# Scores of block-causal attention as three rounded products, from batch 2 on

## The chip, the cores and the metric

The kernel runs on one core of a Trainium2 chip. The metric is the device time of one execution in microseconds. A core has a matrix engine (TensorE, PE in the profile, its weight loads PEld), three engines that work elementwise (VectorE or DVE, ScalarE or ACT, GpSimd or POOL), and SyncE (SP), which here only issues DMAs. Each engine works through its own instructions in order and waits on semaphores for the others. TensorE reads SBUF and writes PSUM, which has 8 banks of 128 rows x 512 f32 values.

## The reference

Attention over 8 batches, 8 heads, 576 positions and a head size of 64, with a mask by blocks of 64; then a feed-forward layer that is gated by a product over positions:

```python
scores = scale * np.matmul(q, k.transpose(0, 1, 3, 2))
mask = block_i >= block_j            # block = pos // 64
scores = np.where(mask, scores, -1000000000.0)
scores = scores - np.max(scores, axis=-1, keepdims=True)
attn = np.exp(scores)
attn = attn / (np.sum(attn, axis=-1, keepdims=True) + 1e-09)
x = np.matmul(attn, v)               # heads side by side: 576 x 512

h = np.maximum(x @ w_in, 0.0)        # 512 -> 1024
u, v = (h[..., :512], h[..., 512:])
v_n = (v - mean(v)) / np.sqrt(var(v) + 1e-06)
v_s = np.einsum('ts,bsd->btd', w_spatial, v_n) + b_spatial[None, :, None]
return (u * v_s) @ w_out             # 512 -> 512
```

## The kernel before

Heads are worked in pairs: head 0 of a pair lies in rows 0 to 63, head 1 in rows 64 to 127, so there are 4 pairs a batch and 32 in all. `raw` holds keys (columns 0 to 575) and queries (576 to 1151) of a pair, head size in the rows. Its pool has two buffers.

Query positions are cut in four tiles `t` = 0 to 3 of 128 and a rest of 64. Tile `t` needs the first 128 (t + 1) keys. `scores_run` (L577) makes the four tiles of a pair with `raw` as f32: for each tile and head one matmul, with 128 queries as the stationary operand and the keys streaming, so 128 to 512 columns with 64 rows. Tiles 3 and 2 take a PSUM bank for each head, tiles 1 and 0 share one. Banks are taken in turn from a ring of six (`bank`, L398), which also serves the rest's scores (`scores_8`, L518, matmuls at L444) and the product with `v` (`av_pair`, L665). Then `top` (L409) takes the maximum with the mask on VectorE (L416) and the exponential on ScalarE (L423), `norm` (L500) divides on GpSimd (L514), and `turn_blocks` (L618) transposes blocks of 32 on VectorE; DMAs on SyncE regroup the result (L652, L660) for `av_pair`.

The feed-forward layer (`moe`, L698) splits each operand into a rounded part and a remainder, both fp32r, and adds three products: rounded with rounded, rounded with remainder, remainder with rounded. Its groups are `v_group` (`mv`, 12 matmuls of 512 columns, 8 for the last), `u_group` (`mu`, 12 of 288), `sp_group` (`ms`, 14 of 288) and `out_group` (`mo`, 12 of 288). Each takes one of two banks (`ps_m`). In `sp_group` VectorE multiplies (L830), ScalarE rounds to `gh` (L833), and a subtraction gives `gl` (L834): on GpSimd for the first three of four groups, on VectorE for the last. `out_group` uses that last part in its last matmul.

From pair 5 on the main loop (L1042) works one pair at a time: `scores_run` of pair g, `av_pair` of pair g - 1, then some 7 or 8 groups of the layer of a batch before, with transposes and regrouping between them. `issue` (L1029) puts out one group, then `follow` (L1023) advances the later stages of the groups before. The rest's scores of pair g + 1 come among the last groups, and after them SyncE loads `v` of pair g + 1 and `raw` of pair g + 2 (L1076 to L1079). `in_order` (L224) fixes each engine's order to that of the program text. By their place in the batch, a pair's groups are: pair 0 the second half's output groups of the batch before that, `v` 0 and 4, `u` 0; pair 1 `v` 1 to 3 and `u` 1 to 4; pair 2 `u` 5 to 7 and the first half's spatial groups; pair 3 the first half's output groups and the second half's spatial groups. Batch 0 differs: its first two output groups stand right behind its first spatial groups, in the stretch of the third pair.

Of the kernel before, what the change touches and what calls it, by code (L numbers as in the profile page):

```python
# [10 lines left out]
F32 = mybir.dt.float32  # L11
F32R = mybir.dt.float32r
I32 = mybir.dt.int32
AF = mybir.ActivationFunctionType
ALU = mybir.AluOpType
PSUM = bass.MemoryType.PSUM

P = 128
S = 576
# [36 lines left out]
def kernel(  # L56
# [10 lines left out]
    nc = tc.nc  # L67
    B, NPAIR = qk.shape[0], qk.shape[1]
# [4 lines left out]
    ND = DH // P  # L73
# [5 lines left out]
    raw_p = ctx.enter_context(tc.tile_pool(name="raw_p", bufs=2))  # L79
# [5 lines left out]
    ff_p = ctx.enter_context(tc.tile_pool(name="ff_p", bufs=1))  # L85
# [122 lines left out]
    raws = {}  # L208

    def load_pair(b, pr):  # L210
        raw = raw_p.tile([P, KQ], F32, tag="raw", name=f"raw_{b}_{pr}")
        if b == 0 and pr == 0:
            for cs in (slice(0, 256), slice(S, S + 256), slice(256, S), slice(S + 256, KQ)):
                nc.sync.dma_start(raw[:, cs], qk[b, pr, :, cs])
        else:
            nc.sync.dma_start(raw, qk[b, pr])
        raws[(b, pr)] = raw


    traced = nc.cur_bb.bb  # L220
# [18 lines left out]
    mm = nc.tensor.matmul  # L239
# [158 lines left out]
    def bank(nm):  # L398
        pool, tag = RING[turn[0] % len(RING)]
        turn[0] += 1  # L400
        return pool.tile([P, 512], F32, tag=tag, name=nm)
# [7 lines left out]
    def top(st, t, hd, p, parts):  # L409

        k = PLACE[(t, hd)]
        at = 0
        for m, ps in enumerate(parts):
            n = ps.shape[1]
            mk = mask[:, 512 - n:] if t < 8 else mask[:, :n]
            nc.vector.tensor_tensor_reduce(  # L416
                out=p[:, at:at + n], in0=ps, in1=mk, scale=-0.125,
                scalar=BIG if m == 0 else st[:, k:k + 1], op0=ALU.add, op1=ALU.min,
                accum_out=st[:, k + m:k + m + 1],
            )  # L420
            at += n
        mx = st[:, k + len(parts) - 1:k + len(parts)]
        nc.scalar.activation(  # L423
            p, p, AF.Exp, bias=mx, scale=-1.0, accum_out=st[:, 10 + k:11 + k]
        )
# [74 lines left out]
    def norm(st, tiles):  # L500
        if tiles[0][0] == 8 and len(tiles) == 2:
            return norm_8(st)
        k0 = PLACE[tiles[0][:2]]
        ks = slice(10 + k0, 10 + k0 + len(tiles))
        rs = slice(20 + k0, 20 + k0 + len(tiles))
        n = len(tiles)
        sums, to = st[:, ks], st[:, 32:32 + n]
        if n > 1:
            sums, to = thrice(sums), three(st[:, 32:32 + 3 * n])
        nc.vector.tensor_scalar(out=to, in0=sums, scalar1=EPS_SM, scalar2=None, op0=ALU.add)  # L510
        nc.vector.reciprocal(st[:, rs], st[:, 32:32 + n])  # L511
        for t, hd, p in tiles:
            k = 20 + PLACE[(t, hd)]
            nc.gpsimd.tensor_scalar(  # L514
                out=p, in0=p, scalar1=st[:, k:k + 1], scalar2=1.0, op0=ALU.mult, op1=ALU.mult
            )
# [60 lines left out]
    def scores_run(b, pr):  # L577


        raw = raws.pop((b, pr))  # L580
        st = stats.pop((b, pr))
        ps = {}
        for t in (3, 2, 1, 0):
            for hd in range(2):
                js = slice(64 * hd, 64 * hd + 64)
                n = P * (t + 1)
                if t:
                    bk = bank(f"s{t}_{b}_{pr}_{hd}")
                    ps[(t, hd)] = bk[:, :n]
                    if t == 1:  # L590
                        ps[(0, hd)] = bk[:, n:n + P]
                mm(  # L592
                    ps[(t, hd)], raw[js, S + t * P:S + (t + 1) * P], raw[js, :n],
                    start=True, stop=True,
                )
        due = None
        for ts in ((3,), (2,), (1, 0)):
            tiles = []
            for hd in range(2):
                p = (p_big if ts[0] == 3 else p_small)(f"p{ts[0]}_{b}_{pr}_{hd}")  # L600
                at = 0
                for t in ts:
                    n = P * (t + 1)
                    p_of[(b, pr, t, hd)] = p[:, at:at + n]
                    top(st, t, hd, p[:, at:at + n], [ps[(t, hd)]])
                    tiles.append((t, hd, p[:, at:at + n]))
                    at += n
            if due:
                norm(st, due)
            due = tiles  # L610
        turn_blocks(b, pr, 8, 0)
        turn_blocks(b, pr, 3, 0)
        norm(st, due)
# [84 lines left out]
    def moe(b):  # L698
# [102 lines left out]
        g = {}  # L801

        def sp_group(z, dc):
            if dc == 0:
                if b == B - 1 and z:

                    t = pt_tile("pb", "g_last", F32R)[:, :2 * ND * HT]
                    t = t.rearrange("p (x d t) -> p x d t", x=2, d=ND)
                    g[z] = (t[:, 0], t[:, 1])
                else:  # L810
                    g[z] = (
                        ff_p.tile([P, ND, HT], F32R, tag="gh", name=f"gh_{b}_{z}"),
                        ff_p.tile([P, ND, HT], F32R, tag="gl", name=f"gl_{b}_{z}"),
                    )
            gh, gl = g[z]
            ps = ps_m.tile([P, 512], F32, tag="m", name=f"ms_{b}_{z}_{dc}")
            zs = slice(z * HT, (z + 1) * HT)
            ds = slice(dc * P, (dc + 1) * P)
            n = 0
            for k in range(FULL):  # L820
                vh, vl = vn[k]
                for (a, w) in ((vh, ws_hi), (vh, ws_lo), (vl, ws_hi)):
                    mm(  # L823
                        ps[:, :HT], a[:, ds], w[:, k, zs], start=(n == 0), stop=False
                    )
                    n += 1
            mm(ps[:, :HT], vs_a[:, ds], ws_a[:, zs], start=False, stop=False)  # L827
            mm(ps[:, :HT], vs_b[:97, ds], ws_b[:97, zs], start=False, stop=True)  # L828
            uz = u_tile()[:, dc, zs]
            nc.vector.tensor_tensor(out=uz, in0=ps[:, :HT], in1=uz, op=ALU.mult)  # L830
            if dc < ND - 1:
                yield
            nc.scalar.copy(gh[:, dc, :], uz)  # L833
            (nc.vector if dc == ND - 1 else nc.gpsimd).tensor_tensor(  # L834
                out=gl[:, dc, :], in0=uz, in1=gh[:, dc, :].bitcast(F32), op=ALU.subtract
            )
            if dc == ND - 1:
                yield
# [23 lines left out]
        out = [[lambda z=z, e=e: out_group(z, e) for e in range(NO)] for z in range(2)]  # L862
# [17 lines left out]
    pairs = [(b, pr) for b in range(B) for pr in range(NPAIR)]  # L880
# [40 lines left out]

    early = steps.pop(-1)
    load_pair(0, 0)
    load_pair(0, 1)
    load_v(0, 0)
# [103 lines left out]
    def issue(f, last=False):  # L1029

        gen = f()
        if not last and step < 28:
            follow()
        next(gen)
        if not last and step >= 28:
            follow()
        behind.append(gen)
        next_step()

    mlp = moe(0)  # L1040
    rest = []
    for g in range(NPAIR, len(pairs)):  # L1042
        b, pr = pairs[g]
        if g > NPAIR:
            scores_run(b, pr)
            av = av_pair(*pairs[g - 1])
            next(av, None)
            turn_blocks(b, pr, 3, 1)
            next(av, None)
            next(av, None)  # L1050
            if pr != 2:
                follow()
            turn_blocks(b, pr, 2, 0)
        regroup_8(b, pr)
        in_order()
        if pr == 0:
            if g > NPAIR:
                mlp = moe(b - 1)
            groups, rest = rest + mlp[0], mlp[-1]
        else:  # L1060
            groups = mlp[pr]
        ahead = scores_8(*pairs[g + 1]) if g + 1 < len(pairs) else iter([])
        for i, f in enumerate(groups):
            issue(f, pr < 2 and i == len(groups) - 1 and not (pr and g > NPAIR + 1))
            if i == 0:
                turn_blocks(b, pr, 1, 0)
                turn_blocks(b, pr, 0, 0)
                turn_blocks(b, pr, 2, 1)
                turn_blocks(b, pr, 1, 1)
                turn_blocks(b, pr, 0, 1)  # L1070
            if i == 1:
                regroup(b, pr)
            if i >= len(groups) - (4 if pr == 0 and g > NPAIR else 3):
                next(ahead, None)
        in_order()
        if g + 1 < len(pairs):  # L1076
            load_v(*pairs[g + 1])
        if g + 2 < len(pairs):
            load_pair(*pairs[g + 2])  # L1079
        in_order()  # L1080
# [61 lines left out]
```

## Time and profile before

| what | us |
|---|---|
| median of 3 runs | 678.1 (677.87 to 678.51) |
| the profiled execution | 677.25 |
| its span in the trace | 675.2 |
| matmuls of the four tiles' scores (L592), 432 records, busy | 65.5 |

The page gives one execution on the chip. Its parts are the busy time of each engine, the span in 40 slices, the DMA queues, the chain of work that ended last (followed back from the last instruction to what released it), the groups of instructions with mean durations, and the DMA issues. In rows of a timeline come the start, the length, the engine with its line, the operation with output and inputs, the shapes, how many were merged, and in brackets the idle time ahead of it with what ended it. The granted clock of TensorE was 0.997 of full speed in this execution.

### The profile page before, as it was taken

Reading aid. Unit: us, or ns where it says so; the run is one execution under the profiler, and the core shown is the slowest. Engines: PE = TensorE matmul, PEld = TensorE weight load, DVE = VectorE, ACT = ScalarE, POOL = GpSimd, SP = SyncE. Lnnn points to the kernel's source line nnn. Section 1 sums busy time; section 2 is a strip of 40 time slices with the busy share of each in tenths; the row PEclk is TensorE's granted clock in tenths of the full one; section 3 lists DMA queues with packets and bytes.
Section 4 is the critical chain, followed back from the end, with each engine's and each line's share of the span. In section 5 each row is a group of like instructions: output and inputs, shape, how many; then the busy total and the mean of one; then the engine's idle time right before and its main releaser. Section 6 shows DMA issues by size and latency. Waiting matters only on the chain.

```text
span 675.2 us, 15538 instructions
## 1 busy us (share of the span) xinstructions
PE 655.9 (97%) x5328; PEld 554.2 (82%) x5328; DVE 482.9 (72%) x1875; ACT 390.8 (58%) x1144; POOL 291.1 (43%) x496
## 2 busy tenths in 40 slices
PE   9887879999999999999999999999999999999998
PEld 5445678888888888988789888888798887999998
DVE  6989899778876687776866788766877768661520
ACT  5977785555943477545754558434775457542632
POOL 4768566343543336442353435433364423640130
PEclk9999989999999999999999999999999999999999
DMA  7534655664557644566656545576445676451002
GB/s 237 164 143 155 190 130 124 177 178 130 143 144 188 155 112 118 160 158 168 152 119 153 147 132 140 146 188 151 111 117 165 153 176 149 113 124 54 0 1 71
DMA packets 51106, 93.45 MB, mean 138 GB/s; under 512 B 5970, under 2 KB 27986, under 8 KB 51028
## 3 DMA queue, kind: packets, MB, share of 16 engines
q1 hardware_dynamic: 41812, 83.03, 48.3%
q10 hardware_dynamic: 9216, 9.44, 4.2%
q8 instruction: 42, 0.69, 0.4%
q14 instruction: 36, 0.29, 0.1%
HBM read 37.13 MB, written 9.44 MB: 69 GB/s over the span
## 4 chain that ended last, share of the span: by engine, by line
PE 74%; DVE 14%; ACT 5%; POOL 3%; issue 2%; SPq 1%; DMA 1%; DVEq 0%; ACTq 0%; POOLq 0%
PE mo L849 16%; PE ms L823 15%; PE mu L793 11%; PE mv L719 8%; PE s L592 8%; PE av L676 7%; DVE p L416 2%; PE s L444 2%; PE mv L730 2%; PE av L688 2%; DVE pb L638 1%; ACT p L423 1%; PE ms L828 1%; PE ms L827 1%; DVE x L329 1%
## 5 line engine op out<-in xcount | busy, mean ns | idle before, releaser
L514 POOL TENSOR_SCALAR p<-p,sst 128x256 f32<-128x256 f32 (+4 forms) x244 | 130.8, 555 | 93.1 <-DVE sst L511 71.3
L423 ACT ACTIVATE p<-p,sst 128x256 f32<-128x256 f32 (+4 forms) x244 | 134.7, 553 | 32.3 <-DVE sst L416 32.2
L793 PE MATMUL mu<-x,wi_hi 128*128 128x288 f32 x512 | 110.9, 300 | 3.4 <-ACT u L798 3.4
L416 DVE CUSTOM_DVE_ANT_0 p<-s,mask 128x512 f32<-128x512 f32 (+1 forms) x216 | 92.5, 484 | 1.3 <-PE s L592 0.7
L793 PEld LDWEIGHTS mu<-x,wi_hi 128*128 128x128 f32 x512 | 85.2, 190 | 8.4 <-ACT u L798 3.9
L638 DVE STREAM_TRANSPOSE pb<-p 128x384 f32<-128x384 f32 (+1 forms) x224 | 89.3, 443 | 0.3 <-POOL p L514 0.3
L719 PE MATMUL mv<-wi_hi,x 128*128 128x512 f32 x256 | 86.9, 401 | 2.4 <-DVE x L329 1.0
L834 POOL TENSOR_TENSOR gl<-u,gh 128x288 fp32r<-128x288 f32 x45 | 36.2, 804 | 112.8 <-ACT gh L833 112.8
L773 POOL TENSOR_TENSOR vl<-vr,vh 128x512 fp32r<-128x512 f32 x32 | 41.3, 1291 | 90.8 <-ACT vh L772 90.8
L830 DVE TENSOR_TENSOR u<-ms,u 128x288 f32<-128x288 f32 x64 | 29.2, 456 | 68.5 <-PE ms L828 68.5
L823 PE MATMUL ms<-ws_hi,vh 128*128 128x288 f32 x256 | 77.1, 301 | 0.2 <-DVE u L830 0.2
L823 PE MATMUL ms<-ws_hi,vl 128*128 128x288 f32 x256 | 75.6, 295 | 0.0
L823 PE MATMUL ms<-ws_lo,vh 128*128 128x288 f32 x256 | 75.4, 294 | 0.0
L793 PE MATMUL mu<-x,wi_lo 128*128 128x288 f32 x256 | 70.4, 297 | 0.0
L676 PE MATMUL av<-ptt,v 128*64 128x64 f32 (+3 forms) x896 | 67.5, 303 | 1.8 <-DVE sst L416 1.8
L676 PEld LDWEIGHTS av<-ptt,v 128*64 128x64 f32 x896 | 53.4, 137 | 15.5 <-DVE sst L416 2.0
L592 PE MATMUL s<-raw 64*128 64x384 f32 (+3 forms) x432 | 65.5, 442 | 0.0
L719 PEld LDWEIGHTS mv<-wi_hi,x 128*128 128x128 f32 x256 | 47.9, 188 | 17.5 <-ACT o L855 2.6
L592 PEld LDWEIGHTS s<-raw 64*128 64x128 f32 x432 | 39.5, 186 | 25.5 <-issue 14.5
L484 ACT ACTIVATE p<-p,sst 128x288 f32<-128x288 f32 x56 | 29.6, 529 | 52.4 <-DVE sst L469 52.3
L855 ACT COPY o<-mo 128x288 f32<-128x288 f32 x64 | 25.6, 399 | 59.3 <-PE mo L849 53.5
L833 ACT CAST gh<-u 128x288 fp32r<-128x288 f32 x60 | 24.3, 428 | 57.3 <-DVE u L830 57.3
(161 smaller groups left out, 1474.3 us busy)
## 6 DMA issues: line engine op xcount, KB each, us to landing
ptt<-pb SPq DMA_DIRECT2D x112, 320.0 KB, 6.1
raw<-qk SPq DMA_DIRECT2D x31, 576.0 KB, 6.3
v<-v SPq DMA_DIRECT2D x32, 320.0 KB, 5.1
outT<-o ACTq DMA_DIRECT2D x64, 144.0 KB, 2.6
ptt<-pb SPq DMA_DIRECT2D x112, 80.0 KB, 2.3
r_gh<-w_in SPq DMA_DIRECT2D x3, 512.0 KB, 4.0
r_gl<-w_in SPq DMA_DIRECT2D x3, 512.0 KB, 3.6
rs<-w_spT SPq DMA_DIRECT2D x4, 288.0 KB, 4.6
```

What stands on the lines that cost most here:

```text
L416: nc.vector.tensor_tensor_reduce(out=p[:, at:at + n], in0=ps, in1=mk, scale=-0.125, scalar=BIG if m == 0 else st[:, k:k + 1], op0=ALU.add, ...
L423: nc.scalar.activation(p, p, AF.Exp, bias=mx, scale=-1.0, accum_out=st[:, 10 + k:11 + k])
L514: nc.gpsimd.tensor_scalar(out=p, in0=p, scalar1=st[:, k:k + 1], scalar2=1.0, op0=ALU.mult, op1=ALU.mult)
L592: mm(ps[(t, hd)], raw[js, S + t * P:S + (t + 1) * P], raw[js, :n], start=True, stop=True,)
L638: nc.vector.transpose(to(hd * XH + 32 * t, [[96, m], *dims] if m > 1 else dims), p[:, :m * P])
L676: mm(to[js, :, 32 * c:], vt[:, c, js], ptt[:, 2 * z:2 * z + 2, at:at + P - 32 * c], start=(c == 0), stop=(c == 3),)
L719: mm(ps, xs[k][:, j, cs], w[:, k, DH:], start=(n == 0), stop=(n == 3 * NC - 1),)
L773: nc.gpsimd.tensor_tensor(out=vl, in0=vr, in1=vh.bitcast(F32), op=ALU.subtract)
L793: mm(ps[:, :HT], w[:, k, ds], xs[k][:, j, zs], start=(n == 0), stop=(n == 3 * NC - 1),)
L823: mm(ps[:, :HT], a[:, ds], w[:, k, zs], start=(n == 0), stop=False)
L834: (nc.vector if dc == ND - 1 else nc.gpsimd).tensor_tensor(out=gl[:, dc, :], in0=uz, in1=gh[:, dc, :].bitcast(F32), op=ALU.subtract)
L849: mm(ps[:, :HT], w[:, k, es], a[:, k, :], start=(n == 0), stop=(n == 3 * ND - 1),)
```

## The change

Pairs 8 to 31 (batch 2 on) get their keys and queries split ahead of their scores. `split_pair` rounds the first 512 keys and queries to fp32r on ScalarE (`hi`), and GpSimd (queries) and VectorE (keys) subtract to get the remainders (`lo`). `hi` lies in the buffer `rw`, which the weights' decoding uses early in the run; `lo` takes a turn in the pool of `raw`. The split of pair g + 1 is put out while pair g's groups run: ahead of the second group in pair 0 of a batch, ahead of the third in the others. `scores_run` then makes three products for each tile and head, which add up in the bank; the two heads alternate within each product. The scores of the rest (`matmuls_8`) still read `raw`. Besides, the last `gl` of `sp_group` moves from VectorE to GpSimd in every batch but the last.

```diff
+    parts = {}
+
+    def split_pair(b, pr):
+
+        hi = ff_p.tile([P, 2, 512], F32R, tag="rw", name=f"hi_{b}_{pr}")
+        lo = raw_p.tile([P, 2, 512], F32R, tag="raw", name=f"lo_{b}_{pr}")
+        raw = raws[(b, pr)].rearrange("p (x s) -> p x s", x=2)[:, :, :512]
+        nc.scalar.copy(hi, raw)
+        for x, engine in ((1, nc.gpsimd), (0, nc.vector)):
+            engine.tensor_tensor(
+                out=lo[:, x], in0=raw[:, x], in1=hi[:, x].bitcast(F32), op=ALU.subtract
+            )
+        parts[(b, pr)] = hi, lo
...
         raw = raws.pop((b, pr))
         st = stats.pop((b, pr))
+        qk = [(raw[:, S:], raw)]
+        if (b, pr) in parts:
+            hi, lo = parts.pop((b, pr))
+            qk = [(x[:, 1], y[:, 0]) for x, y in ((hi, hi), (hi, lo), (lo, hi))]
         ps = {}
         for t in (3, 2, 1, 0):
-            for hd in range(2):
-                js = slice(64 * hd, 64 * hd + 64)
-                n = P * (t + 1)
-                if t:
-                    bk = bank(f"s{t}_{b}_{pr}_{hd}")
-                    ps[(t, hd)] = bk[:, :n]
-                    if t == 1:
-                        ps[(0, hd)] = bk[:, n:n + P]
-                mm(
-                    ps[(t, hd)], raw[js, S + t * P:S + (t + 1) * P], raw[js, :n],
-                    start=True, stop=True,
-                )
+            n = P * (t + 1)
+            for m, (q, k) in enumerate(qk):
+                for hd in range(2):
+                    js = slice(64 * hd, 64 * hd + 64)
+                    if t and m == 0:
+                        bk = bank(f"s{t}_{b}_{pr}_{hd}")
+                        ps[(t, hd)] = bk[:, :n]
+                        if t == 1:
+                            ps[(0, hd)] = bk[:, n:n + P]
+                    mm(
+                        ps[(t, hd)], q[js, t * P:(t + 1) * P], k[js, :n],
+                        start=(m == 0), stop=(m == len(qk) - 1),
+                    )
...
-            (nc.vector if dc == ND - 1 else nc.gpsimd).tensor_tensor(
+            (nc.vector if dc == ND - 1 and b == B - 1 else nc.gpsimd).tensor_tensor(
                 out=gl[:, dc, :], in0=uz, in1=gh[:, dc, :].bitcast(F32), op=ALU.subtract
             )
...
+    SPLIT = (1, 2, 2, 2)
...
         for i, f in enumerate(groups):
+            if i == SPLIT[pr] and 2 * NPAIR <= g + 1 < len(pairs):
+                split_pair(*pairs[g + 1])
             issue(f, pr < 2 and i == len(groups) - 1 and not (pr and g > NPAIR + 1))
```

## The prediction

> **What bounds the kernel now.** I read the page first: the busy shares, then the chain that ended last.
>
> ```profile
> span 675.2 us, 15538 instructions
> PE 655.9 (97%) x5328; PEld 554.2 (82%) x5328; DVE 482.9 (72%) x1875; ACT 390.8 (58%) x1144; POOL 291.1 (43%) x496
> PE 74%; DVE 14%; ACT 5%; POOL 3%; issue 2%; SPq 1%; DMA 1%; DVEq 0%; ACTq 0%; POOLq 0%
> PE mo L849 16%; PE ms L823 15%; PE mu L793 11%; PE mv L719 8%; PE s L592 8%; PE av L676 7%; DVE p L416 2%; PE s L444 2%; PE mv L730 2%; PE av L688 2%; DVE pb L638 1%; ACT p L423 1%; PE ms L828 1%; PE ms L827 1%; DVE x L329 1%
> ```
>
> TensorE is busy nearly always and the chain is mostly its matmuls, the scores of L592 among them with 8%. So TensorE time taken out of L592 shortens the run, unless another chain ends late in that stretch. I looked for such a stretch, first in the windows (one stretch per pair; this one is pair 1 of a batch), then in the chain in order of time.
>
> ```profile
> 391.98:413.26 21.28, 21.20 (x163) 17.23 (x162) 18.44 (x72) 15.20 (x43) 7.01 (x11) 1.00 0.55 141
> ```
>
> ```profile
> 391.98 1.11 PE s L592 x4
> ...
> 404.24 1.30 POOL vl L773
> ...
> 406.21 3.04 PE mv L719 x12
> ```
>
> The columns after the window are its length, then PE, PEld, DVE, ACT and POOL busy. In pair 1 VectorE is busy 18.44 of 21.28 us, and the chain leaves TensorE at 393 and returns only at 406.21, by way of `vl`. There TensorE stands still already. In the stretches of pairs 0, 2 and 3 the chain stays on matmuls.
>
> **The score block, before and after.** One block of L592, from the timeline (start, length, engine, line):
>
> ```profile
> 352.92 0.19 PEld L592 LDWEIGHTS s<-raw 64*128 64x128 f32 x2 [0.16 <-issue]
> 353.45 0.19 PEld L592 LDWEIGHTS s<-raw 64*128 64x128 f32 x2 [0.24 <-issue]
> 353.88 0.19 PEld L592 LDWEIGHTS s<-raw 64*128 64x128 f32 x2 [0.24 <-issue]
> 354.53 0.41 PEld L592 LDWEIGHTS s<-raw 64*128 64x128 f32 x4
> 354.96 0.19 PEld L592 LDWEIGHTS s<-raw 64*128 64x128 f32 x2
> 355.28 0.44 PE L676 MATMUL av<-ptt,v 128*64 128x256 f32 x2
> ```
>
> Each f32 product runs as two passes, and the two heads (rows 0 to 63 and 64 to 127) start together, x2. From 353.45 to 353.88 is one pass of a pair of heads over 512 keys, 0.43. Two passes over 384 take 353.88 to 354.53, 0.325 each; two over 256 take 354.53 to 354.96, 0.215 each. The last 0.32 are two passes over 128 (0.11 each) and 0.10 of changing over to `av`; the first step, 0.53, holds a bare weight load of 0.10. Sum: 0.20 + 2 x (0.43 + 0.325 + 0.215 + 0.11) = 2.36 us a pair.
>
> Afterwards there are three fp32r products of one pass each: 12 steps of two heads instead of 8. The trace shows fp32r only as products that fill the array (97 or 128 rows), never two beside each other:
>
> ```profile
> 398.22 0.39 PE L719 MATMUL mv<-wi_lo,x 128*128 128x512 f32 x1
> 398.45 0.62 PE L719 MATMUL mv<-wi_hi,x 128*128 128x512 f32 x2
> 398.90 0.39 PE L719 MATMUL mv<-wi_lo,x 128*128 128x512 f32 x1
> ```
>
> ```profile
> 390.40 1.58 PE mu L793 x12
> ```
>
> At 512 it is (398.90 - 398.22) / 3 = 0.227 a matmul, at 288 1.58 / 12 = 0.132. A line through both gives 0.173 at 384, 0.118 at 256 and 0.064 at 128. The last is open: a weight load stands before each matmul, and with 128 columns it can be longer than the pass.
>
> ```profile
> L793 PEld LDWEIGHTS mu<-x,wi_hi 128*128 128x128 f32 x512 | 85.2, 190 | 8.4 <-ACT u L798 3.9 <-issue 2.6 <-ACT vs_a L779 0.4
> L592 PEld LDWEIGHTS s<-raw 64*128 64x128 f32 x432 | 39.5, 186 | 25.5 <-issue 14.5 <-DVE st L761 1.4 <-DVE st L753 1.0
> ```
>
> An fp32r load is no shorter than an f32 one (190 against 186 ns), so I take 0.11, the nearest row, the f32 pass over 128. New block: 0.20 + 3 x (0.227 + 0.173 + 0.118 + 0.11) = 2.08 us. That is **0.27 us** less for each pair; with 0.064 at 128 it is 0.41. That two fp32r heads run together is not in the trace; I take it from the f32 heads, which do, and price the contrary below.
>
> The Trainium skill ("TensorE: Matmul & The Clock Gate", Weight-path perf modes) says that fast weight load comes on with 128 weight columns and a type other than FP32. The 190 ns row speaks against that for fp32r; by the rule the gain a pair would be the 0.41.
>
> **Which pairs keep it.** 24 pairs change (batches 2 to 7), six in each place.
>
> ```profile
> 392.82 0.18 DVE L742 BATCH_NORM_AGGREGATE st<-st 128x2 f32<-128x6 f32 x1
> 415.16 0.08 DVE L416 DVE_READ_ACCUMULATOR2_ANT sst<- 128x1 f32 x1
> ```
>
> Pair 1 keeps little. VectorE finishes L742 at 393.00 and starts the first maximum at 393.07; scores that come earlier move it by 0.07 at most. From there VectorE is dense up to `vl`, which frees the `vr` buffer that the `mv` of 406.21 waits for. So TensorE arrives 0.27 earlier and waits 0.20 longer: gain 0.07. In pair 2 the first maximum is done at 415.24, and its bank is the one that `av` takes next; the new scores would end at 413.19 + 2.08 = 415.27, a wait of some 0.02: gain 0.25. Pairs 0 and 3 keep 0.27, the more so as `gl` no longer stands ahead of their first maximum.
>
> **The split.** It adds one ACT copy of 1024 columns, one POOL and one DVE subtraction of 512.
>
> ```profile
> L833 ACT CAST gh<-u 128x288 fp32r<-128x288 f32 x60 | 24.3, 428 | 57.3 <-DVE u L830 57.3
> L772 ACT CAST vh<-vr 128x512 fp32r<-128x512 f32 x32 | 19.9, 620 | 1.0
> ```
>
> ```profile
> L780 DVE TENSOR_TENSOR vs_a<-vr,vs_b 64x512 fp32r<-64x512 f32 x8 | 5.5, 686 | 0.3
> L834 DVE TENSOR_TENSOR gl<-u,gh 128x288 fp32r<-128x288 f32 x15 | 6.9, 458 | 7.5 <-ACT gh L833 7.5
> ```
>
> ```profile
> L773 POOL TENSOR_TENSOR vl<-vr,vh 128x512 fp32r<-128x512 f32 x32 | 41.3, 1291 | 90.8 <-ACT vh L772 90.8
> ```
>
> The slope is (620 - 428) / 224 = 0.857 ns a column, so the copy takes 620 + 512 x 0.857 = 1.06 us; DVE 0.69, POOL 1.29. All three queues run in order, so I looked for the idle time where each lands (in brackets), for pairs 0, 1, 2, 3 in turn, ACT first:
>
> ```profile
> 381.78 0.40 ACT L855 COPY o<-mo 128x288 f32<-128x288 f32 x1 [1.19 <-PE mo L849]
> 405.56 0.60 ACT L724 ACTIVATE vr<-mv 128x512 f32<-128x512 f32 x1 [1.40 <-POOL vl L773]
> 423.56 0.41 ACT L798 ACTIVATE u<-mu 128x288 f32<-128x288 f32 x1 [1.12 <-PE mu L793]
> 442.18 0.40 ACT L855 COPY o<-mo 128x288 f32<-128x288 f32 x1 [1.25 <-DMA outT<-o]
> ```
>
> ```profile
> 385.63 0.46 DVE L477 CUSTOM_DVE_ANT_0 p<-s,mask 128x288 f32<-128x288 f32 x1 [1.82 <-PE s L444]
> 407.31 0.42 DVE L778 CAST vs_b<-vr 64x512 fp32r<-64x512 f32 x1 [1.47 <-ACT vr L766]
> 425.43 0.46 DVE L830 TENSOR_TENSOR u<-ms,u 128x288 f32<-128x288 f32 x1 [1.37 <-PE ms L828]
> 445.57 0.46 DVE L830 TENSOR_TENSOR u<-ms,u 128x288 f32<-128x288 f32 x1 [2.90 <-PE ms L828]
> ```
>
> Every hole holds its piece. In pairs 0 and 3 the issue of an output DMA (0.34) lies in ACT's hole too, so the next eviction comes about 0.25 late; its bank is wanted only a group later (1.58), so TensorE sees nothing. In pair 1 the copy falls between `vh` and L724, which waits for POOL anyway, and POOL's part comes behind `vl`. Behind the waiting DVE subtraction stand the next maximum or `u` product, which are not ready. I cost the split at nothing. Without that cover, the copy's 1.06 ahead of an eviction with about 0.8 to spare would cost 0.26 a pair.
>
> Loads: the remainder takes the second `raw` buffer, so the load on SyncE waits for the last reader, L444, and is read at the copy, not first at L444.
>
> ```profile
> 372.21 0.46 SPq L216 DMA_DIRECT2D raw<-qk  x1
> ```
>
> ```profile
> raw<-qk SPq DMA_DIRECT2D x31, 576.0 KB, 6.3
> ```
>
> It is there at 378.5; pair 0's copy comes at about 381, behind the eviction ahead of 381.78. Cover 2.4 us: nothing.
>
> **Last gl on GpSimd.** 14 subtractions go from DVE (0.46) to POOL (0.80). Only batch 0 has its `mo` right behind `ms`:
>
> ```profile
> 116.39 0.82 POOL L834 TENSOR_TENSOR gl<-u,gh 128x288 fp32r<-128x288 f32 x1 [2.21 <-ACT gh L833]
> ```
>
> ```profile
> 117.77 0.29 PE L849 MATMUL mo<-gl,wo_hi 128*128 128x288 f32 x1
> ```
>
> The new one would run 117.2 to 118.0, while TensorE wants it at 117.77: 0.3 lost once. Elsewhere scores and `av` (4.4 us) lie between; nothing.
>
> **Sum.** 12 x 0.27 + 6 x 0.25 + 6 x 0.07 - 0.3 = 4.9 us. The profiled execution took 677.25 (span 675.2 and 2.05 around it), 0.85 below the median of 678.1. Less 4.9 it becomes 672.4, and the median **673.2**.
>
> **Rivals.**
> - Heads not together (slower). If fp32r uses the array one head at a time, the 12 steps become 24: 6 x (0.227 + 0.173 + 0.118 + 0.064 to 0.11) = 3.5 to 3.8 against 2.16 now, some 1.5 more a pair; pair 1 hides 0.26 of it in its present stall. 18 x 1.5 + 6 x 1.24 + 0.3 = 34.7: 713. It decides from a second head that starts 0.27 / 12 = 0.02 us late in each step. For it: every fp32r row here fills the array. Against: f32 heads start within a hundredth of a us. Chance 0.13; a milder form, weight loads of both heads in turn (0.21 a step), gives 3 x (0.227 + 3 x 0.21) = 2.57, 0.41 more a pair: 687, chance 0.05.
> - Cover lost: 0.26 a pair as above eats the gain: 678, chance 0.14: 0.08 of it within 0.2%, 0.03 on either side.
> - Three quarters: three passes at half of an f32 record, 3 x (0.215 + 0.163 + 0.108 + 0.055) = 1.62, saves 0.54. Pair 1 keeps 0.07 and pair 2 0.25: 12 x 0.54 + 1.5 + 0.4 - 0.3 = 8.1, giving 670.0. Against it are the 0.227 and the weight load. Chance 0.10. The Trainium skill ("FP8 and Floating Point Precision", TensorE Precision Notes) has "True FP32: 4 passes", so three products cost three quarters; the trace's 0.86 for f32 against 4 x 0.227 agrees roughly.
> - It does less than it says: L592 would not grow from 16 to 24 records in 24 pairs. Excluded by the code, no chance given.
>
> **Chances.** Forecast 0.58 (its own range 671.7, with 0.064 at 128, to 675.5). A measurement here can tell 0.2%, 1.4 us, from no change. Faster 0.58 + 0.10 + 0.03 = 0.71; same 0.08; slower 0.13 + 0.05 + 0.03 = 0.21. The range runs from 669.5 (three quarters) to 679.5 (cover lost) and leaves out 0.18, the two slow heads' cases.
>
> **What would show it.** L592 with 24 records a pair in about 2.08 us, the two heads' starts under 0.01 apart and the 128-key steps at 0.11; the `mv` of pair 1 waiting 0.2 longer for L724; ACT's copy at 1.06 with no wait of PE on ACT behind it. Wrong would be: heads that alternate, PE waiting for `hi` or `lo`, or an `av` that waits for the first maximum in every pair.

## The result and the profile after

The changed kernel takes 672.36 us (median of 4 runs, 670.72 to 673.57), the kernel before 677.99 (median of 4, 677.36 to 678.51). The ratio is 0.9916, with a 95% interval of 0.9892 to 0.9940. The profiled execution took 670.72 us with a span of 668.9, against 677.25 and 675.2. From the page of the changed kernel, the same four rows as of before:

```profile
span 668.9 us, 16105 instructions
PE 647.2 (97%) x5520; PEld 561.5 (84%) x5520; DVE 501.9 (75%) x1885; ACT 414.4 (62%) x1168; POOL 334.5 (50%) x534
PE 67%; DVE 16%; issue 5%; POOL 5%; ACT 5%; DMA 1%; DVEq 0%; POOLq 0%; ACTq 0%
PE ms L842 15%; PE mo L868 15%; PE mu L812 8%; PE mv L738 8%; PE av L695 7%; PE s L611 5%; DVE p L430 3%; POOL p L528 2%; PE s L458 2%; ACT p L437 2%; PE mv L749 2%; PE av L707 2%; DVE pb L657 1%; POOL vl L792 1%; PE ms L847 1%
```

TensorE is as full as before, in a shorter span, and the scores (now L611) fall from 8% of the chain to 5%. The other engines do 19, 24 and 43 us more work, and more of the chain runs through them. The lines of the changed kernel are some 19 higher than before: L611 was L592, L430 was L416, L738 was L719, L695 was L676.

One score block, from timelines of TensorE and of its weight loads cut small (start, length, engine and line, operation, x how many; the window of the last row of L611 ends between the two heads, so it shows one of them). It belongs to the same pair as 413.19 of before, a pair 2:

```profile
408.99 0.50 PE L611 MATMUL s<-hi 64*128 64x512 f32 x2
409.33 0.39 PE L611 MATMUL s<-lo,hi 64*128 64x512 f32 x2
409.56 0.39 PE L611 MATMUL s<-hi,lo 64*128 64x512 f32 x2
409.79 0.33 PE L611 MATMUL s<-hi 64*128 64x384 f32 x2
410.31 0.28 PE L611 MATMUL s<-hi 64*128 64x256 f32 x2
410.65 0.23 PE L611 MATMUL s<-hi 64*128 64x128 f32 x2
410.71 0.28 PE L611 MATMUL s<-lo,hi 64*128 64x128 f32 x2
410.83 0.27 PE L611 MATMUL s<-hi,lo 64*128 64x128 f32 x1
411.12 0.20 PEld L695 LDWEIGHTS av<-ptt,v 128*64 128x64 f32 x4 [0.17 <-DVE sst L430]
```

The heads start together: over all 24 changed blocks the two starts of a step lie at most 0.01 us apart. A step is 0.23 at 512 keys (409.56 to 409.79), 0.173 at 384 (three from 409.79 to 410.31), 0.115 at 256 (three from 410.31 to 410.65), and at 128 once 0.06 and once 0.12. The loads of `av` then stand idle for 0.17, and VectorE's maximum ends that.

I took the start of each block and the start of the `av` behind it from both traces and averaged them by the pair's place in its batch (times in us; pairs 8 to 30, 5 or 6 of each place):

| place | scores to av, before | after | from block to block, before | after | forecast gain | gain |
|---|---|---|---|---|---|---|
| pair 0 | 2.36 | 2.05 | 18.90 | 18.58 | 0.27 | 0.32 |
| pair 1 | 2.36 | 2.04 | 21.33 | 21.09 | 0.07 | 0.24 |
| pair 2 | 2.36 | 2.14 | 18.58 | 18.37 | 0.25 | 0.21 |
| pair 3 | 2.36 | 2.04 | 20.09 | 19.78 | 0.27 | 0.31 |

One of the six stretches of pair 1 before was 21.62; the others were 21.27 or 21.28, so its gain is 0.18 but for that one. From the first changed block to the last the traces hold 453.32 us (136.49 to 589.81) before and 447.15 (135.86 to 583.01) after: 6.17 us for 23 pairs, all of the change in the medians and a little more. The granted clock was 1.00 over this whole stretch in both traces, so the clock has no part in it.

### The profile page after: what moved, and what is told of

Its sections match the earlier page's. It is cut to its first block, busy times and chain, and to the rows that moved or that the text cites. A ratio compares the mean times of both kernels' runs of the same rounds, so it can differ in the third digit from the quotient of the medians.

```text
span 668.9 us, 16105 instructions
## 1 busy us (share of the span) xinstructions
PE 647.2 (97%) x5520; PEld 561.5 (84%) x5520; DVE 501.9 (75%) x1885; ACT 414.4 (62%) x1168; POOL 334.5 (50%) x534
## 4 chain that ended last, share of the span: by engine, by line
PE 67%; DVE 16%; issue 5%; POOL 5%; ACT 5%; DMA 1%; DVEq 0%; POOLq 0%; ACTq 0%
PE ms L842 15%; PE mo L868 15%; PE mu L812 8%; PE mv L738 8%; PE av L695 7%; PE s L611 5%; DVE p L430 3%; POOL p L528 2%; PE s L458 2%; ACT p L437 2%; PE mv L749 2%; PE av L707 2%; DVE pb L657 1%; POOL vl L792 1%; PE ms L847 1%
## 5 line engine op out<-in xcount | busy, mean ns | idle before, releaser
L430 DVE CUSTOM_DVE_ANT_0 p<-s,mask 128x512 f32<-128x512 f32 (+1 forms) x216 | 92.4, 484 | 7.1 <-PE s L611 6.8
L738 PE MATMUL mv<-wi_hi,x 128*128 128x512 f32 x256 | 86.7, 401 | 3.0 <-ACT vr L743 1.4
L853 POOL TENSOR_TENSOR gl<-u,gh 128x288 fp32r<-128x288 f32 x59 | 46.8, 804 | 82.6 <-ACT gh L852 82.6
L695 PE MATMUL av<-ptt,v 128*64 128x64 f32 (+3 forms) x896 | 67.5, 303 | 2.0 <-DVE sst L430 1.8
L695 PEld LDWEIGHTS av<-ptt,v 128*64 128x64 f32 x896 | 53.4, 137 | 15.0 <-DVE sst L430 3.0
L738 PEld LDWEIGHTS mv<-wi_hi,x 128*128 128x128 f32 x256 | 47.9, 188 | 18.0 <-ACT vr L743 2.8
L842 PEld LDWEIGHTS ms<-ws_hi,vh 128*128 128x128 f32 x256 | 48.3, 189 | 6.9 <-DVE u L849 6.1
L868 PE MATMUL mo<-gh,wo_hi 128*128 128x288 f32 x240 | 53.3, 303 | 0.2 <-ACT gh L852 0.2
```

The source lines that it names most:

```text
L430: nc.vector.tensor_tensor_reduce(out=p[:, at:at + n], in0=ps, in1=mk, scale=-0.125, scalar=BIG if m == 0 else st[:, k:k + 1], op0=ALU.add, ...
L695: mm(to[js, :, 32 * c:], vt[:, c, js], ptt[:, 2 * z:2 * z + 2, at:at + P - 32 * c], start=(c == 0), stop=(c == 3),)
L738: mm(ps, xs[k][:, j, cs], w[:, k, DH:], start=(n == 0), stop=(n == 3 * NC - 1),)
L842: mm(ps[:, :HT], a[:, ds], w[:, k, zs], start=(n == 0), stop=False)
L853: (nc.vector if dc == ND - 1 and b == B - 1 else nc.gpsimd).tensor_tensor(out=gl[:, dc, :], in0=uz, in1=gh[:, dc, :].bitcast(F32), op=ALU. ...
L868: mm(ps[:, :HT], w[:, k, es], a[:, k, :], start=(n == 0), stop=(n == 3 * ND - 1),)
```

## The experiments

**Is it the move of gl?** Two kernels: the change with the last `gl` back on VectorE, and the kernel before with only that move.

```diff
-            (nc.vector if dc == ND - 1 and b == B - 1 else nc.gpsimd).tensor_tensor(
+            (nc.vector if dc == ND - 1 else nc.gpsimd).tensor_tensor(
```

> The changed kernel with the last gl back on VectorE in every batch; the rest as changed. Theory A (the gain is TensorE's own: score blocks of 2.04 us instead of 2.36, the move of gl only keeps VectorE out of the way): the first maximum in pairs 0 and 3 starts behind gl, some 1.45 us after the scores' start, its bank comes free at 2.19, and av waits 0.1 to 0.2 us in 12 stretches: 1.2 to 2.4 us back, 673.5 to 675. Theory B (the move of gl brought a good part of the gain): 676 or more. Theory C (the move did nothing for the gain): 672.4 as changed.

Measured: 673.86 us, ratio to before 0.9949 (0.9935 to 0.9962). Blocks of pairs 0 and 3 took 2.19 us instead of 2.04, those of pairs 1 and 2 stayed. A block of pair 3 in this kernel, first its start, then VectorE, then the chain:

```profile
429.79 0.19 PEld L611 LDWEIGHTS s<-hi 64*128 64x128 f32 x2 [0.16 <-issue]
```

```profile
430.86 0.46 DVE L853 TENSOR_TENSOR gl<-u,gh 128x288 fp32r<-128x288 f32 x1 [0.50 <-ACT gh L852]
431.23 0.68 DVE L430 CUSTOM_DVE_ANT_0 p<-s,mask 128x512 f32<-128x512 f32 x1
```

```profile
431.98 2.40 PE av L695 x32
```

`gl` waits for ScalarE and holds the first maximum behind it; `av`, which takes that maximum's bank, starts at 2.19. Twelve stretches that are 0.14 to 0.15 longer make 1.7 us. The medians differ from those of the change by 1.5, and the two intervals just overlap.

> The kernel before with nothing but the last gl moved to GpSimd in all batches but the last. Theory A: 678.0, within 0.5 us of before, with TensorE waiting some 0.2 us more once in batch 0. Theory B: 676.5 or less. Both: the first maximum in pairs 0 and 3 starts 0.3 us or more earlier.

```diff
-            (nc.vector if dc == ND - 1 else nc.gpsimd).tensor_tensor(
+            (nc.vector if dc == ND - 1 and b == B - 1 else nc.gpsimd).tensor_tensor(
```

Measured on the kernel before: 677.29 us, ratio 0.9997 (0.9989 to 1.0006). By itself the move brings nothing. The first maximum of pairs 0 and 3 does start earlier, 1.16 us after the scores' start instead of 1.44, but the f32 scores end at 2.36, after the bank is free either way. The move is worth its 1.7 us only beside the shorter scores, since it takes away what would be late next.

**Does the split cost anything?** Two kernels again: the split without the products, and the products without the split.

```diff
         if (b, pr) in parts:
             hi, lo = parts.pop((b, pr))
-            qk = [(x[:, 1], y[:, 0]) for x, y in ((hi, hi), (hi, lo), (lo, hi))]
```

> The changed kernel with the split put out as before the scores, but the scores computed from raw in f32, so that hi and lo are written and never read. Theory A (the split is hidden behind TensorE): 678.0, within 0.7 us of before. Theory D (the split costs time that the shorter scores outweigh, since VectorE's and GpSimd's subtractions hold each other up, 1.5 to 1.9 us instead of 0.7 and 1.3): 0.1 to 0.2 us in each of 24 stretches, 680.5 to 683.

Measured: 677.24 us, ratio 0.9993 (0.9985 to 1.0002).

```diff
-            if i == SPLIT[pr] and 2 * NPAIR <= g + 1 < len(pairs):
+            if i == SPLIT[pr] and g + 1 == 2 * NPAIR:
...
-        lo = raw_p.tile([P, 2, 512], F32R, tag="raw", name=f"lo_{b}_{pr}")
...
-        for x, engine in ((1, nc.gpsimd), (0, nc.vector)):
-            engine.tensor_tensor(
-                out=lo[:, x], in0=raw[:, x], in1=hi[:, x].bitcast(F32), op=ALU.subtract
-            )
-        parts[(b, pr)] = hi, lo
+        parts[(b, pr)] = hi, hi
...
-        if (b, pr) in parts:
-            hi, lo = parts.pop((b, pr))
+        if b > 1:
+            hi, lo = parts[(2, 0)]
```

> The changed kernel with the copy hi made once, for the first pair of batch 2, and no subtraction at all; every later pair multiplies that one copy three times (queries and keys of the first pair instead of its own, hi in place of lo). The products keep their number, type and size. Theory A: 672.4, within 1 us of the changed kernel. Theory D: 2.5 to 5 us less, 667.5 to 670.

Measured: 672.75 us, ratio 0.9925 (0.9912 to 0.9937), as the change itself. From both sides the split costs nothing that can be told: from the first changed block to the last, the trace with the unused split holds 452.85 us against 453.32 before, and the one with the split made once 447.44 against 447.15 with the change. Yet its subtractions were slower than I had costed them. From the changed kernel, the two rows of L228 among its instructions (shortest, median and longest in ns), then timelines of GpSimd and of VectorE in a pair 1:

```profile
L228 DVE TENSOR_TENSOR lo<-raw,hi x24: 648/694/1869, 129.7 to 575.4; 128x512 fp32r<-128x512 f32 x24
L228 POOL TENSOR_TENSOR lo<-raw,hi x24: 1269/1294/1798, 129.7 to 575.4; 128x512 fp32r<-128x512 f32 x24
```

```profile
401.30 1.27 POOL L228 TENSOR_TENSOR lo<-raw,hi 128x512 fp32r<-128x512 f32 x1
```

```profile
401.59 1.54 DVE L228 TENSOR_TENSOR lo<-raw,hi 128x512 fp32r<-128x512 f32 x1
403.13 0.42 DVE L797 CAST vs_b<-vr 64x512 fp32r<-64x512 f32 x1
```

VectorE's piece begins at 401.59, while GpSimd's runs until 402.57, and ends 0.56 after it, while the fastest of these subtractions take 0.65 in all. So it seems to have stood still for most of GpSimd's time and then done its work. It was done just when L797 could begin.

**One instruction for both remainders.**

```diff
-        for x, engine in ((1, nc.gpsimd), (0, nc.vector)):
-            engine.tensor_tensor(
-                out=lo[:, x], in0=raw[:, x], in1=hi[:, x].bitcast(F32), op=ALU.subtract
-            )
+        nc.vector.tensor_tensor(
+            out=lo, in0=raw, in1=hi.bitcast(F32), op=ALU.subtract
+        )
```

> The changed kernel with both remainders in one VectorE instruction of 1024 columns, GpSimd doing nothing for the split. By the slope of VectorE's own rows about 1.22 us where nothing stands in its way, against 0.65 to 1.87 for the 512 columns now. Theory A (all of it lies in holes of 1.4 us and more): 672.4 within 1 us. Theory D: faster, since the two subtractions no longer hold each other up, by 1 us or more.

Measured: 672.75 us, ratio 0.9914 (0.9899 to 0.9929), no difference from the change that these runs can tell, so theory D falls here too. With GpSimd out of it, all 24 subtractions take the same time, for twice the columns:

```profile
L227 DVE TENSOR_TENSOR lo<-raw,hi x24: 1177/1182/1225, 131.1 to 577.3; 128x1024 fp32r<-128x1024 f32 x24
```

**What is hidden behind the scores?** One product instead of three.

```diff
-            qk = [(x[:, 1], y[:, 0]) for x, y in ((hi, hi), (hi, lo), (lo, hi))]
+            qk = [(hi[:, 1], hi[:, 0])]
```

> The changed kernel with one product (hi by hi) instead of three in pairs 8 to 31; the remainders are still computed. It leaves 16 of 24 matmuls of a score block out. If TensorE alone set the time, each block would take 0.20 + 0.62 = 0.8 us instead of 2.04 and 24 pairs would save 29 us: 643. Theory A with the waits on the first maximum: av takes the bank of the first maximum, which is done about 1.3 us after the scores' start where VectorE is free (pairs 0 and 3), so these keep some 0.6 us; pairs 1 and 2, where VectorE is dense, keep 0 to 0.1 us: 12 x 0.6 to 0.7, so 664 to 666.

Measured: 665.84 us, ratio 0.9816 (0.9803 to 0.9828); it is the fastest of all. Blocks took 1.29 us in pairs 0 and 3, 1.73 in pair 1 and 2.14 in pair 2. Pair 2 is at its floor already with three products: its first maximum starts 1.37 to 1.41 us after the scores' start before, with the change and here. Pair 1 has a shorter block, but its stretch is 21.06 against 21.09. Pair 0 keeps 0.75 in five of its six stretches. Pair 3 keeps only 0.18 on average (stretches of 19.02 to 20.22), where I had expected 0.6: its shorter block moves the waiting further on. The waits of TensorE's loads, in total, times, longest:

```profile
PEld av L695 <- DVE sst L430: 23.8, 25, 2.0
```

With three products the same row says 3.0, 7, 2.0. Two thirds of the score work taken out is 24 x 2/3 x (2.04 - 0.20) = 29 us of TensorE. Of these 6.5 came through by the medians, 4.7 by the two traces from the first changed block to the last. So the forecast time came out, but by other shares of the pairs than I had given.

**Must the heads alternate?** The loops over heads and products exchanged, then heads outermost.

```diff
-            for m, (q, k) in enumerate(qk):
-                for hd in range(2):
+            for hd in range(2):
+                for m, (q, k) in enumerate(qk):
```

> The changed kernel with the loops over heads and products exchanged: the three products of head 0, then those of head 1, the same matmuls in another order. Theory A (two fp32r products of 64 rows in the two halves of the array run at the same time, and only because they stand next to each other): most steps of a pair fall apart, five of six neighbours share a half, a block takes 3 to 3.7 us instead of 2.04, 695 to 710. Rival (the order doesn't matter, the engine finds the other half's matmul by itself): 672.4.

Measured: 672.95 us (2 runs), ratio 0.9923 (0.9906 to 0.9940); blocks took 2.05 us as in the change. My expectation fell. In the program the second head's first product comes third after the first head's, and on the chip it starts with it:

```profile
411.17 0.50 PE L611 MATMUL s<-hi 64*128 64x512 f32 x2
411.50 0.40 PE L611 MATMUL s<-lo,hi 64*128 64x512 f32 x2
```

```diff
-        for t in (3, 2, 1, 0):
-            n = P * (t + 1)
-            for m, (q, k) in enumerate(qk):
-                for hd in range(2):
+        for hd in range(2):
+            for t in (3, 2, 1, 0):
+                n = P * (t + 1)
+                for m, (q, k) in enumerate(qk):
```

> The changed kernel with the loop over heads outermost: all 12 matmuls of head 0, then all 12 of head 1. Theory F (each half of the array takes its own matmuls in order and starts the other head's well ahead of the program's order, as with 3 matmuls between them): a block stays at 2.05 us and the total near 672.4. Theory G (the engine looks only a few instructions ahead): the heads come apart, a block takes 2.3 to 3.5 us, the second head's first maximum comes later too, 680 to 705.

Measured: 710.02 us (2 runs), ratio 1.0476 (1.0455 to 1.0497); a block takes 3.62 us, a little beyond theory G's range. The unsplit pairs 5 to 7 are reordered too. The steps come single until head 0 has three matmuls left; then head 1's first one, of 512 keys, joins them (TensorE's rows, the first and those around the change):

```profile
411.40 0.50 PE L611 MATMUL s<-hi 64*128 64x512 f32 x1
...
412.96 0.49 PE L611 MATMUL s<-hi 64*128 64x512 f32 x2
413.13 0.27 PE L611 MATMUL s<-lo,hi 64*128 64x128 f32 x1
413.24 0.27 PE L611 MATMUL s<-hi,lo 64*128 64x128 f32 x1
413.29 0.39 PE L611 MATMUL s<-lo,hi 64*128 64x512 f32 x1
```

The row at 412.96 merges head 1's product over 512 keys with head 0's first one over 128, which the trace has 0.1 later. The order of the banks changes with this edit as well, but a wait for a bank doesn't explain the delay: neither head 1's first load nor its matmul has idle time ahead that another engine ended. So the halves work beside each other if the other half's matmul stands about three places ahead, and not if it stands twelve ahead. Distances between these two were not tried.

**What holds pair 1?** A fourth buffer of `vr`, so that the third `v_group` need not wait for `vl`. One kernel makes room for it by dropping a buffer of `o`.

```diff
-    o_p = ctx.enter_context(tc.tile_pool(name="o_p", bufs=2))
+    o_p = ctx.enter_context(tc.tile_pool(name="o_p", bufs=1))
...
-            vr = ff_p.tile([P, DH], F32, tag="vr", name=f"vr_{b}_{c}", bufs=3)
+            vr = ff_p.tile([P, DH], F32, tag="vr", name=f"vr_{b}_{c}", bufs=4)
```

> The changed kernel with four buffers of vr instead of three, and one of o instead of two to make room. In pair 1 the third v_group's eviction need no longer wait for vl. Theory A (that wait is what pair 1 loses of its gain): the mv in pair 1 no longer waits, 0.3 to 0.45 us less in six stretches and as much in batch 1, minus what one buffer of o costs: 669.5 to 671. Rival (VectorE is the bound of pair 1 by itself): 672.4 or more.

Measured: 733.52 us, ratio 1.0829 (1.0791 to 1.0867). The total tells nothing of `vr`, since the other edit drowned it:

```profile
ACT o L874 <- DMA outT<-o: 130.0, 45, 6.5
```

Of the 64 evictions of an output 45 waited for the write of the one before, 130 us together. The outputs lie in the stretches of pairs 0 and 3, which grew to 23.4 and 24.1 us on average (five of them had a granted clock of 0.83 to 0.93). The stretches of pairs 1 and 2 hold none, and there `vr` can be read after all: 20.64 against 21.09, and 18.73 against 18.37. The other kernel takes the room from the decoding's scratch tile.

```diff
-    scaled = const.tile([P, NC, P], F32, name="scaled")
...
+            scaled = ff_p.tile([P, DH], F32, tag="vr", name="scaled", bufs=4).rearrange("p (c n) -> p c n", c=NC)
             nc.scalar.mul(scaled, high.bitcast(F32), 2.0**-112)
...
-            vr = ff_p.tile([P, DH], F32, tag="vr", name=f"vr_{b}_{c}", bufs=3)
+            vr = ff_p.tile([P, DH], F32, tag="vr", name=f"vr_{b}_{c}", bufs=4)
```

> The changed kernel with four buffers of vr and the two of o kept; the room comes from the decoding's scratch tile, which takes a turn among the vr buffers and so may delay batch 0 a little. Theory A (pair 1 keeps only 0.18 of 0.31 us since its third v_group's eviction waits for vl, at the end of a chain on VectorE): the mv behind it starts 0.3 to 0.45 us earlier, pair 1's stretch falls from 21.09 to 20.7, six or seven times: 669.5 to 670.5. Rival (VectorE is itself the bound of pair 1, buffer or not): the stretch stays at 21.09 and the wait turns up later in it, or in pair 2; 672.4.

Measured: 669.96 us, ratio 0.9889 (0.9873 to 0.9904). That beats the kernel before; against the change the intervals overlap. Pair 1's stretch fell from 21.09 to 20.61, but pair 2's rose from 18.37 to 18.75, its block from 2.14 to 2.52, which leaves 0.1 us a batch. From the first changed block to the last it is 446.70 us against 447.15. The larger part lies ahead of it: the three pairs before the first changed block take 56.59 us against 57.83, although the granted clock was 0.92 in the first of them and 1.00 with the change. So the forecast time came out partly by luck, since pair 1's gain was mostly lost again in pair 2. Both theories had a part: the wait for `vl` went, and the next one stood right behind it. From this kernel, `av` of pair 2, then VectorE in pair 1 ahead of it:

```profile
409.95 0.14 PEld L695 LDWEIGHTS av<-ptt,v 128*64 128x64 f32 x2 [0.54 <-DVE sst L430]
```

```profile
400.51 1.55 DVE L228 TENSOR_TENSOR lo<-raw,hi 128x512 fp32r<-128x512 f32 x1
401.99 0.41 DVE L797 CAST vs_b<-vr 64x512 fp32r<-64x512 f32 x1
```

Now VectorE has no hole left, and the split's subtraction, held up by GpSimd's, is a link of the chain. A split by one engine alone beside the four buffers was not tried.

> One product (hi by hi; it leaves 16 of 24 matmuls of a score block out) together with the four buffers of vr. With one product alone pairs 1 and 2 kept 0.03 and 0.0 us of the shorter scores (stretches of 21.06 and 18.37). Theory A: freed of the wait for vl, pair 1's stretch falls by 0.4 to 0.8 us: 662 to 664. Rival (VectorE is the bound of pair 1): 665.8 as with one product alone.

Measured (the edits of both): 667.91 us, ratio 0.9862 (0.9845 to 0.9878). The expected 662 to 664 did not come, and the median lies above that of one product alone. The clock has a part in that: it was granted at 0.987 to 0.992 in these four runs, against 0.995 to 1.000 with one product alone. In the trace two of the six stretches of pair 2 had a granted clock of 0.92 and took 20.5 us; the other four, at 1.00, took 18.80 to 18.85. At the full clock, then, pair 1's stretch fell from 21.06 to 20.51 and pair 2's rose from 18.37 to 18.83, which again leaves 0.1 us a batch. Why the clock fell in these runs is not shown.

## Why the prediction was right, by its steps

**Total.** 673.2 forecast, 672.4 measured; 4.9 us less forecast, 5.6 measured. The likeliest case came true, and its terms were each off by a little. The same sum with the measured terms, 6 x 0.32 + 6 x 0.31 + 6 x 0.21 + 6 x 0.18 - 0.42, gives 5.7. That the total came so close is in part luck: pairs 0, 1 and 3 kept more than forecast, pair 2 less, and the loss by `gl` was larger.

**The step durations** by a line through the fp32r rows of 512 and 288 columns held: 0.227, 0.173, 0.118 forecast, 0.23, 0.173, 0.115 measured, two heads at a time. The mis-sized one was 128 keys. I took the f32 row, 0.11, for all three, and the first took 0.06. In the block above, the three loads for 128 keys start at 410.54, 410.66 and 410.77, so 0.11 to 0.12 apart, and the first of them still beside the last step of 256 keys; that leaves the first step shorter. The Trainium skill's rule on fast weight load ("TensorE: Matmul & The Clock Gate", Weight-path perf modes) doesn't explain it: fp32r loads in L611 last 0.18 to 0.19 us as the f32 ones did. A block of 2.04 instead of 2.08 makes the gain of pairs 0 and 3 0.31 instead of 0.27.

**Pair 1** kept 0.18 to 0.24 where I gave it 0.07. I had read the end of L742 as the earliest start of the first maximum. In the changed kernel:

```profile
388.81 0.18 DVE L761 BATCH_NORM_AGGREGATE st<-st 128x2 f32<-128x6 f32 x1
388.91 0.67 DVE L430 CUSTOM_DVE_ANT_0 p<-s,mask 128x512 f32<-128x512 f32 x1
```

The maximum starts 0.10 after the start of the instruction ahead (0.25 before), and 0.08 before its end, so these overlap: 1.01 us after the scores' start (387.90) instead of 1.16 (391.91 to 393.07). The chain from there to `mv` is as forecast, and it moved by that 0.15. TensorE's stop ahead of `mv` did grow; the waits for L743 come to 2.8 us for its load and 1.4 for the matmul, against 2.3 and 0.4 for L724 before. That is 0.47 a time for the load, against 0.32 in five of the six before: 0.15 longer where I gave 0.20.

**Pair 2** kept 0.21 of 0.25. The place was right, the size small: the first maximum ended at 411.07, and `av` began at 411.12, not in the same moment.

**The gl term** was there and a little larger, 0.42 us where I gave 0.3. In batch 0 the first output group takes 2.72 us from its first matmul to that of the next group, 2.30 before, and 2.71 with the move of `gl` alone. The changed kernel's waits of TensorE's loads have it (total, times, longest):

```profile
PEld mo L868 <- POOL gl L853: 0.5, 1, 0.5
```

I had the order on GpSimd the other way round. The moved subtraction runs first (115.02 to 115.82), and behind it the third spatial group's (115.78 to 116.58), which the output group wants earlier, in its ninth matmul. The three pairs that hold it can't show the loss as a whole, 58.01 us before and 57.83 with the change: in the first of them the granted clock was 0.93 before and 1.00 with the change. What the prediction had only in half a sentence weighs more: the move was needed to hold pairs 0 and 3 at their full gain, 1.7 us by the kernel without it.

**The split at nothing** held, from both sides. Its copy took 1.04 to 1.05 us (1.06 forecast). Its subtractions reached 1.87 and 1.80 us instead of 0.69 and 1.29, because I had costed the two engines as if they didn't touch. The Trainium skill ("SBUF — State Buffer", Terms) has it that VectorE and GpSimd share a pair of SBUF ports that one instruction holds to its end while the other engine stands still. The 0.56 us of work behind GpSimd's end, and the even 1.18 us without GpSimd, agree. That rule speaks against splitting at once on both, and I had not weighed it; here the holes were wide enough. With four buffers of `vr` they no longer were.

**The rivals.** Heads not together: excluded by the two starts, 0.01 us apart at most in every step. Its price came near all the same, 713 against 710.0 in the kernel that forces the heads apart, although there a few steps still overlap. Cover lost: excluded by the two kernels on the split. Three quarters: excluded by the block, 2.04 and not 1.82.

## What to carry to other kernels

Price a matmul by its passes and its weight load from rows of its own type, then ask at each place what releases the instruction behind it: a shorter block keeps its gain only as far as the next bank or buffer is free. An edit that brings nothing alone can be what lets another one keep its gain, so try it in both directions, alone and taken out of the whole. Where a wait is removed, the next one may stand within a few tenths of a us.

## What the hardware showed that I had not expected

Matmuls of 64 rows in different halves of the array start in another order than the program's. With two others between them they started together, within 0.02 us in all 24 blocks; with eleven between them only when three of the first head were left. The Trainium skill ("TensorE: Matmul & The Clock Gate", Part 3, The mechanism) says that matmuls start and end in the program's order and only weight loads are taken ahead. The records of these two runs show otherwise, and the block of 2.05 us with the heads apart could not be that short if it held.
